# Filling matmuls in a backward recurrence, and four moves of copies and loads in its forward recurrence

One core of one Trainium2 chip (trn2). The metric is the device time of one execution in microseconds (us), lower is better. The kernel before takes 5632.72 us, the median of 3 runs (5621.08 to 5634.92).

## The reference

A block of attention with a carried memory, gated by a feed-forward branch, with the gradients of all its inputs. Cut to what matters here:

```python
def _A_ref(x, mem0, Wq, Wk, Wv, Wo, seg_len):      # S = 2048, Dm = 640, H = 32 heads of 128, M = 8, seg_len = 32
    mem = mem0
    for s in range(n_seg):                          # 64 segments, one after the other
        h = concat([mem, x[segment s]])             # 40 rows
        q, k, v = h @ Wq, h @ Wk, h @ Wv
        p = softmax(mask(q @ k.T * scale))
        o = (p @ v) @ Wo
        mem = o[:, :M]                              # 8 rows go on to the next segment
        outs.append(o[:, M:])
# result: x + A(layernorm(x)) * silu(B(layernorm(x)));  the kernel also returns the gradients of x, mem0 and all weights
```

Only the 8 memory rows depend on the segment before. So the kernel runs two recurrent loops of 64 steps, one forward for the memory rows and one backward for their gradients, and puts the work of the other rows, in units of four heads of three segments ("x units"), into the gaps of each step.

## The kernel before

A step is a chain of matmuls and copies with named gaps W0, W1, W2 and G1 to G6. A function called at each gap adds filling work.

Forward loop, the parts that the change touches:

```python
WARM = dict(G2=1, G3=1, G4=2, G5=1)             # filling matmuls, 512 columns each, result never read
def gap(g):
    FILL(g, t, at, kbatch)
    for i in range(WARM.get(g, 0)):
        nc.tensor.matmul((bA if g == "G4" else bB)[:], k.ident[:], Wq[:, 0, 0:512], start=True, stop=True)
    if g in ("G2", "G5"):                       # transposes of one weight block on PE ...
        wt["u"] = units.pop(0); wt["p"] = bview(bA if g == "G2" else bB, ...); wt["u"][0](wt["p"])
    if g == "G2": turned('v', nc.sync)          # ... and their copy, by VectorE
    if g == "G6": turned('s', nc.sync)          # ... or by ScalarE
def FILL(g, t, at, kbatch):
    if g == "W0":
        ... at(pv, t - 1, 0); at(turn_p, t - 1, 2)
        for u in kb[0:2]: ld_k(*u)              # key rows, two loads on SyncE's queue
    elif g == "W1": at(pv, t - 1, 1)
    elif g == "W2": at(pv, t - 1, 2); ride_ld(t + 1)    # third x unit
    elif g == "G1": oride(t); at(scores, t, 0); at(turn_q, t, 2); ...
    # ... cut ...
def oride(t):                                   # GpSimd: the o rows of the other segment tokens
    nc.gpsimd.tensor_copy(oTm[:, :, 8:32], uu.pop(("o", t))[:])
def pv(tl, qd, q=nc.gpsimd):
    # PE: xot and xpo;  ScalarE: copies xoT and xv, and the issue of xoT's store between them;
    q.dma_start(k.OR[...], v[0:n])              # GpSimd's queue: waits for xv
# the memory chain between the gaps (cut):
#   W2 -> psT matmuls -> sTm copy (ScalarE) -> ride copy (GpSimd) -> gap G1 -> transposes -> msb (VectorE)
#   -> Em = exp (ScalarE) -> Zm, rZm, Pm = Em * rZm (VectorE) -> gap G2 -> transposes of Pm -> PTm -> gap G3
#   -> poms -> oTm (VectorE) -> gap G4 -> projection with Wo -> fold -> next step
```

Backward loop:

```python
WARM = dict(G1=1, G5=2, G6=1)
# gap W1: turn(t, 1) (transposes of the second unit's v and gradient rows), gmem_ld(t + 1, 2)
# gap G3: turn(t, 2), dprob(t, 1);   after it: load_k(t - 1), two pairs of dSm stores
# gap G4: load_xp(t - 1), dsoft(t, 1), gmem_ld(t, 0)
# gap G5: dprob(t, 2), gmem_ld(t, 1)
def gmem_ld(tl, qd):
    gmem(tl, qd)        # last use of a unit's buffers (gkp matmuls), store GXP on SyncE's queue
    ld_next()           # load of the unit four further on: gqv (3 to 5 loads), gor, gPr, SyncE's queue
```

A unit's load reuses the buffers that the `gmem` four units earlier frees. Backward steps have three, three and two units in turn (t mod 3 = 0, 2, 1; t runs from 63 down to 0).

Of the kernel before, what the change touches and what calls it, by code (L numbers as in the profile page):

```python
# [10 lines left out]
F32 = mybir.dt.float32  # L11
# [5 lines left out]
P = 128  # L17
# [385 lines left out]
def phase3_Afwd(k, W4, Wv, Wk_):  # L403
    nc, tc = k.nc, k.tc
# [5 lines left out]
    with tc.tile_pool(name="b0", bufs=1) as io, tc.tile_pool(name="b0s", bufs=3) as stp, \  # L410
# [7 lines left out]
        n = 0  # L418
# [22 lines left out]
    with tc.tile_pool(name="ast", bufs=1) as st, tc.tile_pool(name="achain", bufs=1) as ch, \  # L441
# [247 lines left out]
        def oride(t):  # L689
            if 0 <= t - k.OT0 < k.NO:  # L690
                nc.gpsimd.tensor_copy(oTm[:, :, 8:32], uu.pop(("o", t))[:])

        def pv(tl, qd, q=nc.gpsimd):
            n = k.geo(tl)[3]
            c0 = qd * 512
            v = uu.pop(("v", tl, qd))
            if 4 * tl < k.NO:
                pt = ps.tile([P, 4, 96], F32, name="xot", tag="x", bufs=5)
                for j in range(4):
                    nc.tensor.matmul(pt[:, j, :], v[0:n, j * P:(j + 1) * P], PTs[qd % 2][0:n, j, 24:120], start=True, stop=True)  # L700
                ot = fl.tile([P, 4, 4, 24], BF16, name="xoT", tag="xoT", bufs=2)
                nc.scalar.copy(ot[:].rearrange("p c h t -> p h c t"), pt[:].rearrange("p h (c t) -> p h c t", t=24))
                nc.scalar.dma_start(k.OTX[4 * tl:4 * tl + 4, :, 4 * qd:4 * qd + 4, :].rearrange("c p h t -> p c (h t)"),
                                    ot[:].rearrange("p c h t -> p c (h t)"))
            po = ps.tile([P, 512], F32, name="xpo", tag="x", bufs=5)
            for j in range(4):
                nc.tensor.matmul(po[:, j * P:(j + 1) * P], PTs[qd % 2][0:n, j, :], v[0:n, j * P:(j + 1) * P],
                                 start=True, stop=True)
            nc.scalar.copy(v[0:n], po[0:n])  # L709
            q.dma_start(k.OR[120 * tl:120 * tl + n, c0:c0 + 512], v[0:n])  # L710

# [17 lines left out]
        def turned(eng, q):  # L729
            wt["u"][1](fl.tile([P, DC, P], BF16, name="wTst", tag="wTst"), wt["p"], eng, q)  # L730

        def gap_of(t):
            def at(f, tt, i):
                b = batch.get(tt, ())
                if i < len(b):
                    f(*b[i])

            def gap(g):
                FILL(g, t, at, kbatch)
                for i in range(WARM.get(g, 0)):  # L740
                    nc.tensor.matmul((bA if g == "G4" else bB)[:], k.ident[:], Wq[:, 0, 0:512], start=True, stop=True)

                if g in ("G2", "G5"):
                    wt["u"] = units.pop(0)
                    wt["p"] = bview(bA if g == "G2" else bB, P, DC, P, bf=True)
                    wt["u"][0](wt["p"])
                if g == "G2":
                    turned('v', nc.sync)
                if g == "G6":
                    turned('s', nc.sync)  # L750
            return gap

        def FILL(g, t, at, kbatch):
            kb = kbatch.get(t, ())
            if g == "W0":
                oride_ld(t)
                at(pv, t - 1, 0)
                at(turn_p, t - 1, 2)
                for u in kb[0:2]:
                    ld_k(*u)  # L760
            elif g == "W1":
                at(pv, t - 1, 1)
            elif g == "W2":
                at(pv, t - 1, 2)
                ride_ld(t + 1)
            elif g == "G1":
                oride(t)
                at(scores, t, 0)
                at(turn_q, t, 2)
                for i in range(2):  # L770
                    at(lambda a, b: ld("q", a, b), t + 1, i)
            elif g == "G2":
                at(scores, t, 1)
                at(scores, t, 2)
                for u in kb[0:2]:
                    kprep(*u)
                for u in kb[2:]:
                    ld_k(*u)
                for i in range(3):
                    at(lambda a, b: ld("v", a, b), t, i)  # L780
            elif g == "G3":
                at(soft, t, 0)
                at(soft, t, 1)
            elif g == "G4":
                at(soft, t, 2)
                for i in range(3):
                    at(norm, t, i)
            elif g == "G5":
                at(turn_p, t, 0)
                at(turn_q, t + 1, 0)  # L790
                at(lambda a, b: ld("q", a, b), t + 1, 2)
            elif g == "G6":
                at(turn_p, t, 1)
                at(turn_q, t + 1, 1)
                for u in kb[2:]:
                    kprep(*u)
# [184 lines left out]
def phase4_Abwd(k, out2, WoT, WvT, WkT, WqT, later):  # L981
# [3 lines left out]
    with tc.tile_pool(name="gst", bufs=1) as st, tc.tile_pool(name="gchain", bufs=1) as ch, \  # L985
# [20 lines left out]
        nc.sync.dma_start(k.m_rows(k.GWO, T - 1).rearrange("r (c d) -> (r c) d", d=160),  # L1006
                          goxs[(T - 1) % 2][0:32].rearrange("p a b -> p (a b)"))
        rides = {}
        WARM = dict(G1=1, G5=2, G6=1)

        def ride_ld(t):
            if t < 8:
# [245 lines left out]
        def gap_of(t):  # L1258
# [5 lines left out]
            def gap(g):  # L1264
# [21 lines left out]
                elif g == "G6":  # L1286
                    at(dsoft, t, 2)
                for i in range(WARM.get(g, 0)):
                    nc.tensor.matmul((bA if g[0] == "W" or g == "G1" else bB)[:], k.ident[:], WqT[:, 0, 0:512], start=True, stop=True)
            return gap  # L1290
        todo = pro + todo

# [713 lines left out]
```

## Time and profile before

| | before |
|---|---|
| median time, us | 5632.72 |
| forward loop, first to 64th step start, us | 1354.6 (half speed 68) |
| backward loop, first to 64th step start, us | 1260.6 (half speed 187) |
| mean backward step, us | 20.01 |
| mean granted TensorE clock | 0.946 |

The step starts are the first matmul of each step that reads the carried rows; "half speed" is time at a granted clock of 0.5 in the profile. The granted clock is 1.0 or 0.5 there, nothing between, and it changes on a grid of 3.41 us: of its 186 stretches in the kernel before, all but the last are multiples of 3.413 us. The lines of the profile that carry the argument stand in the prediction: the busy times of the two loops, steps with and without half speed, and the waits in a step.

### The profile page before, as it was taken

How to read it: one execution, taken by the hardware profiler on the slowest of the kernel's cores; microseconds unless marked ns; L12 is line 12 of the kernel's file. 1: busy time of each engine (PE TensorE's matmuls, PEld its weight loads, DVE VectorE, ACT ScalarE, POOL GpSimd, SP SyncE). 2: the span in 40 equal slices, each digit the busy share in tenths (PEclk: the TensorE clock that was granted, in tenths of full speed). 3: DMA queues.
4: the chain of work that ended last, by engine and by line, in shares of the span. 5: the costliest groups of instructions: out<-in, count | busy, mean ns of one | idle time of the engine just before them, and what ended most of it. 6: DMA issues, size and time to landing. Idle time of an engine off the chain costs nothing. (4 is left out here: it accounts for less than half of the span.)

```text
span 5628.0 us, 166669 instructions
## 1 busy us (share of the span) xinstructions
PE 4974.2 (88%) x67201; PEld 3195.0 (57%) x67486; DVE 2378.9 (42%) x7485; ACT 1834.3 (33%) x5040; POOL 1566.2 (28%) x2606
## 2 busy tenths in 40 slices
PE   4988889899888775889888896999999999999999
PEld 2554555555555453556666564665566556657565
DVE  5742555555555423444445442332233223311461
ACT  2432455555555522323333331332223212301111
POOL 0000244444444303333333332342234223300000
PEclk9999999999999787989999997999999999999999
DMA  7563455556555475666666664444344334456332
GB/s 256 181 205 94 140 163 168 167 166 170 161 157 151 113 208 164 177 185 182 188 179 179 174 173 114 120 100 98 84 108 102 99 87 102 122 163 228 102 118 91
DMA packets 1007171, 835.83 MB, mean 149 GB/s; under 512 B 505131, under 2 KB 894919, under 8 KB 1003083
## 3 DMA queue, kind: packets, MB, share of 16 engines
q1 hardware_dynamic: 760275, 570.63, 35.7%
q0 software_dynamic: 92560, 149.71, 9.5%
q10 hardware_dynamic: 153564, 104.81, 6.5%
q8 instruction: 532, 8.72, 0.6%
q14 instruction: 240, 1.97, 0.1%
HBM read 511.81 MB, written 324.39 MB: 149 GB/s over the span
## 5 line engine op out<-in xcount | busy, mean ns | idle before, releaser
L1460 PE MATMUL wg<-gr,hr 120*128 120x512 bf16 (+1 forms) x2640 | 588.1, 384 | 17.3 <-DVE dST L1392 13.2
L1438 PE MATMUL g<-w,gT 128*128 128x320 bf16 x3840 | 547.9, 299 | 0.0
L1460 PEld LDWEIGHTS <-hr 120*128 120x128 bf16 (+1 forms) x2640 | 257.8, 99 | 339.5 <-issue 45.9
L1438 PEld LDWEIGHTS <-gT 128*128 128x128 bf16 x3840 | 368.6, 98 | 136.0
L251 POOL DMA_DIRECT2D r<-GOS x256 | 143.1, 564 | 794.1 <-PE r6p L1402 720.5
L370 PEld LDWEIGHTS <-gkv 128*8 128x8 bf16 x8192 | 213.6, 98 | 152.1 <-DVE gkv L1069 34.4
L90 DVE CAST wgo<-wg 128x512 bf16<-128x512 f32 x72 | 47.5, 687 | 583.3 <-PE wg L1460 292.1
L351 PEld LDWEIGHTS <-hx 128*32 128x32 bf16 x7680 | 180.1, 96 | 182.7 <-issue 30.9
L90 DVE CAST stg<-bank 128x512 bf16<-128x512 f32 x256 | 177.0, 691 | 224.2 <-PE bank L351 213.6
L661 ACT ACTIVATE xP<-xsp,xnm 120x120 bf16<-120x120 f32 (+1 forms) x704 | 239.9, 375 | 32.1 <-issue 25.6
L370 PE MATMUL gbank<-WvT,gkv 128*8 128x320 bf16 x4096 | 225.6, 396 | 27.4 <-DVE gkv L1069 27.4
L1447 DVE TENSOR_TENSOR ghacc<-ghacc,g 128x320 f32<-128x320 f32 x240 | 117.0, 487 | 277.2 <-PE g L1438 277.2
L92 ACT CAST wgo<-wg 128x512 bf16<-128x512 f32 x48 | 25.8, 589 | 635.5 <-PE wg L1460 635.5
L1405 ACT CAST gr<-r6p 120x512 bf16<-120x512 f32 (+1 forms) x176 | 103.1, 586 | 361.2 <-PE r6p L1402 339.6
L1220 POOL DMA_DIRECT2D DSR<-gdS x176 | 101.6, 577 | 419.1 <-DVE gdS L1218 370.1
L710 POOL DMA_DIRECT2D OR<-xv x163 | 93.3, 572 | 444.2 <-ACT xv L709 280.8
L672 POOL TENSOR_TENSOR xP<-xP,xrz 120x480 bf16<-120x480 bf16 x163 | 161.6, 992 | 162.1 <-ACT xP L661 108.0
L92 ACT COPY gT<-t6g 128x960 bf16<-128x960 bf16 (+5 forms) x216 | 166.8, 792 | 118.4 <-PE t6g L1421 117.9
L370 PE MATMUL bank<-Wo,oTm 128*32 128x320 bf16 x4032 | 177.7, 330 | 14.7 <-DVE oTm L579 13.5
L1218 DVE SCALAR_TENSOR_TENSOR gdS<-gdp,Dx,gPr 120x120 bf16<-120x120 f32 (+1 forms) x680 | 182.9, 331 | 0.0
L536 DVE COPY vt<-stg 8x512 bf16<-8x512 bf16 x512 | 166.1, 324 | 31.8 <-ACT stg L92 24.9
L370 PEld LDWEIGHTS <-oTm 128*32 128x32 bf16 x4032 | 138.6, 105 | 64.9 <-issue 41.0
(360 smaller groups left out, 11094.4 us busy)
## 6 DMA issues: line engine op xcount, KB each, us to landing
QVS<-stg SPq DMA_DIRECT2D x128, 256.0 KB
gqv<-QVS SPq DMA_DIRECT2D x108, 192.0 KB
vTt<-VTD SPq DMA_DIRECT2D x64, 320.0 KB
VTD<-gvT POOLq DMA_DIRECT2D x168, 120.0 KB, 3.4
OR<-xv POOLq DMA_DIRECT2D x163, 120.0 KB, 2.8
DSR<-gdS POOLq DMA_DIRECT2D x168, 112.5 KB, 3.2
dS<-DSR SPq DMA_DIRECT2D x168, 112.5 KB
P<-PR SPq DMA_DIRECT2D x168, 112.5 KB
```

The lines of the kernel that those rows point to most:

```text
L90: return nc.vector.tensor_copy(out, in_)
L92: return nc.scalar.copy(out, in_)
L251: eng.dma_start(d, src if src.shape[0] > 1 else src[0])
L351: k.nc.tensor.matmul(bank[32 * g:32 * g + 32, :], x[:, dc, :], W[:, dc, c0:c0 + 512], start=(dc == 0), stop=(dc == k.DC - 1), tile_positio ...
L370: k.nc.tensor.matmul(pm[p0:p0 + nq, 0:320], x[:, h, :], W[:, h, 320 * b:320 * b + 320], start=(first and i == 0), stop=(last and i == 15), ...
L536: nc.vector.tensor_copy(vt[p0:p0 + 8, c0:c0 + 512], sv[32 * g:32 * g + 8, b * 512:(b + 1) * 512])
L661: nc.scalar.activation(Pb[0:n, j, 0:n], sp[0:n, j, :], ACT.Exp, bias=nmx[0:n, j:j + 1], scale=k.scale, accum_out=Z[0:n, j:j + 1])
L672: eng.tensor_tensor(Pb[0:n, :, 0:n], Pb[0:n, :, 0:n], bc_last(rz[0:n], n), ALU.mult)
L1218: nc.vector.scalar_tensor_tensor(dS[0:n, j, :], dp[0:n, j, :], Dx[0:n, j:j + 1], Pr[0:n, j, :], op0=ALU.subtract, op1=ALU.mult)
L1438: nc.tensor.matmul(pg[:], ring[:, i, j, r0:r0 + P], Ws[qd][i][:, j, 320 * h:320 * h + 320], start=(i == 0 and j == 0), stop=(i == 2 and j ...
L1447: nc.vector.tensor_tensor(a if qd < 7 else gx[:, 320 * h:320 * h + 320], a, g[h][:], ALU.add)
L1460: nc.tensor.matmul(accs[dc][:], hr[0:n, tl, dc * P:(dc + 1) * P], st["g", NTL * qd + tl, i][0:n, :], start=(tl == 0), stop=(tl == NTL - 1))
```

## The change

In the backward loop, matmuls that compute nothing used are to keep PE busy enough for its full clock. In the forward loop, four moves: VectorE's copy of a weight block goes behind the softmax starts; the third unit's copies go behind the memory scores' copy; ScalarE's copy of a weight block goes ahead of the q and k copies of G6; key rows are loaded after the key store.

```diff
@@ forward loop
+        def pv_mm(tl, qd):      # the matmuls of pv
+        def pv_out(tl, qd, q=nc.gpsimd):    # xoT copy and store, xv copy and store
             def gap(g):
+                if g == "G6":
+                    turned('s', nc.sync)
                 FILL(g, t, at, kbatch)
+                if g == "G3":
+                    turned('v', nc.sync)
                 ... filling matmuls, weight transposes ...
-                if g == "G2":
-                    turned('v', nc.sync)
-                if g == "G6":
-                    turned('s', nc.sync)
         def FILL(g, t, at, kbatch):
                 at(turn_p, t - 1, 2)
+            elif g == "W1":
                 for u in kb[0:2]:
                     ld_k(*u)
-            elif g == "W1":
                 at(pv, t - 1, 1)
             elif g == "W2":
-                at(pv, t - 1, 2)
+                at(pv_mm if t < T else pv, t - 1, 2)
             elif g == "G1":
+                at(pv_out, t - 1, 2)
                 oride(t)
@@ backward loop
-        WARM = dict(G1=1, G5=2, G6=1)
+        WARM = dict(W1=3, G1=2, G2=2, G5=2, G6=1)
-                    nc.tensor.matmul((bA if g[0] == "W" or g == "G1" else bB)[:], ...
+                    nc.tensor.matmul((bA if g in ("W1", "G1", "G2") else bB)[:], ...
```

The rest of the diff splits `pv` into `pv_mm` and `pv_out`.

More of the change, by code (lines that the diff above doesn't have):

```diff
@@ L693, in pv @@
         def pv(tl, qd, q=nc.gpsimd):
+            pv_mm(tl, qd)
+            pv_out(tl, qd, q)
+        def pv_mm(tl, qd):
             n = k.geo(tl)[3]
-            c0 = qd * 512
-            v = uu.pop(("v", tl, qd))
+            v = uu["v", tl, qd]
             if 4 * tl < k.NO:
@@ L700, in pv @@
                     nc.tensor.matmul(pt[:, j, :], v[0:n, j * P:(j + 1) * P], PTs[qd % 2][0:n, j, 24:120], start=True, stop=True)
+                uu["pt", tl, qd] = pt
+            po = ps.tile([P, 512], F32, name="xpo", tag="x", bufs=5)
+            for j in range(4):
+                nc.tensor.matmul(po[:, j * P:(j + 1) * P], PTs[qd % 2][0:n, j, :], v[0:n, j * P:(j + 1) * P],
+                                 start=True, stop=True)
+            uu["po", tl, qd] = po
+        def pv_out(tl, qd, q=nc.gpsimd):
+            n = k.geo(tl)[3]
+            c0 = qd * 512
+            v, po = uu.pop(("v", tl, qd)), uu.pop(("po", tl, qd))
+            if 4 * tl < k.NO:
+                pt = uu.pop(("pt", tl, qd))
                 ot = fl.tile([P, 4, 4, 24], BF16, name="xoT", tag="xoT", bufs=2)
@@ L704, in pv @@
                                     ot[:].rearrange("p c h t -> p c (h t)"))
-            po = ps.tile([P, 512], F32, name="xpo", tag="x", bufs=5)
-            for j in range(4):
-                nc.tensor.matmul(po[:, j * P:(j + 1) * P], PTs[qd % 2][0:n, j, :], v[0:n, j * P:(j + 1) * P],
-                                 start=True, stop=True)
             nc.scalar.copy(v[0:n], po[0:n])
@@ L1288, in gap @@
                 for i in range(WARM.get(g, 0)):
-                    nc.tensor.matmul((bA if g[0] == "W" or g == "G1" else bB)[:], k.ident[:], WqT[:, 0, 0:512], start=True, stop=True)
+                    nc.tensor.matmul((bA if g in ("W1", "G1", "G2") else bB)[:], k.ident[:], WqT[:, 0, 0:512], start=True, stop=True)
             return gap
```

## The prediction

> **What bounds the kernel now.** I read the page first, then the granted clock by stage, then single steps of the two recurrent loops, the waits in each loop, and the timelines of ACT and PE inside a step. Each loop has 64 steps, every one fed by the step before, so a loop costs 64 times its step.
>
> The busy times and clock of the forward loop (first row) and the backward loop (second); the columns are time, busy us of PE, PEld, DVE, ACT and POOL (instruction counts in brackets), granted PE clock, DMA share, GB/s:
> ```profile
> 542.60:1907.00 1364.40, 1225.12 (x22711) 764.23 (x22836) 763.65 (x2228) 737.19 (x2455) 550.69 (x783) 0.98 0.55 158
> 2205.50:3470.00 1264.50, 1126.41 (x24102) 749.08 (x24229) 589.78 (x2769) 378.13 (x1227) 419.01 (x765) 0.93 0.63 170
> ```
> See the clock: 0.98 forward, 0.93 backward. Now five successive steps of the backward loop, cut where the first matmul of a step starts, and below them two neighbouring stretches of 3.41 us inside the fifth, and two pairs of such stretches elsewhere:
> ```profile
> 3027.67:3046.15 18.48, 16.39 (x379) 11.29 (x381) 9.95 (x50) 5.60 (x19) 6.44 (x13) 1.00 0.63 175
> 3046.15:3064.97 18.82, 16.77 (x386) 11.63 (x389) 8.60 (x41) 6.38 (x20) 6.62 (x13) 1.00 0.70 184
> 3064.97:3085.23 20.26, 18.38 (x395) 12.36 (x398) 10.30 (x53) 6.68 (x22) 7.13 (x14) 0.92 0.67 191
> 3085.23:3105.23 20.00, 17.91 (x379) 11.65 (x382) 10.04 (x50) 5.60 (x19) 6.43 (x13) 0.91 0.64 181
> 3105.23:3125.74 20.51, 18.45 (x386) 12.34 (x389) 8.70 (x41) 6.39 (x20) 6.61 (x13) 0.92 0.59 157
> ...
> 3109.24:3112.66 3.42, 2.14 (x54) 1.76 (x58) 1.22 (x5) 1.57 (x5) 1.29 (x2) 1.00 0.77 237
> 3112.66:3116.07 3.41, 3.41 (x60) 1.94 (x56) 2.80 (x17) 0.00 (x0) 0.21 (x1) 0.50 0.58 165
> ...
> 3051.22:3054.63 3.41, 2.74 (x75) 2.05 (x76) 1.62 (x8) 0.63 (x2) 0.47 (x1) 1.00 0.56 176
> 3054.63:3058.04 3.41, 3.41 (x96) 2.68 (x92) 3.35 (x24) 1.68 (x5) 1.26 (x3) 1.00 0.84 256
> ```
> See two things. A step at full clock takes 18.5 or 18.8 us; one in which the clock stood at one half for 3.41 us takes 20.0 to 20.5. And the half-speed stretch follows a stretch with little PE work: 2.14 us busy, against 2.74 where the clock stayed. I sorted all 3.41 us stretches of the loop so: nearly all that led to half speed had under about 2.45 us of PE, and 42 of 46 began 2.5 to 4.3 us into the step. There PE waits three times (a step at full clock, us and length first, idle time and its releaser last):
> ```profile
> 3050.77 1.00 PE L1090 MATMUL gbank<-gmT,vTt 128*40 128x8 bf16 x32 [0.89 <-DVE gmT L1085]
> 3052.49 0.29 PE L1067 MATMUL gbank<-bdP,gOst 128*128 128x128 bf16 x2 [0.23 <-ACT gOst L1098]
> 3053.36 0.31 PE L370 MATMUL gbank<-WvT,gkv 128*8 128x320 bf16 x4 [0.43 <-DVE gkv L1069]
> ```
> These are the ends of gaps W1, G1 and G2, where the change puts its fillers. The forward loop is bound by a chain PE, ACT, DVE. ACT in a step with three x units, one early in the loop, then the waits of the whole forward loop that matter (us, times, longest):
> ```profile
> 1151.90 0.49 ACT L702 CAST xoT<-xot 128x384 bf16<-128x384 f32 x1
> 1152.41 0.37 ACTq L703 DMA_DIRECT2D OTX<-xoT  x1
> 1152.95 0.58 ACT L709 CAST xv<-xpo 120x512 bf16<-120x512 f32 x1 [0.57 <-DMA OR<-xv]
> 1153.43 0.36 ACT L543 CAST sTm<-bank 40x256 bf16<-40x256 f32 x1
> 1153.70 0.55 ACT L631 COPY xqT<-qpt 128x480 bf16<-128x480 bf16 x1
> 1154.72 0.27 ACT L557 ACTIVATE Em<-msb 128x80 bf16<-128x80 f32 x1 [0.47 <-DVE msb L555]
> ```
> ```profile
> ACT stg L92 <- DMA KS<-stg: 17.9, 19, 2.2
> PE bank L351 <- ACT wTst L92: 9.6, 38, 0.6
> ```
> The memory scores end on PE at 1152.76, but their copy sTm starts at 1153.43, behind the third unit's two copies and a DMA issue. The value stage buffer waits 19 times for the key store, and the second key half 38 times for the weight transpose's copy.
>
> [...] a window need not be idle, 2.1 to 2.4 us of PE in 3.41 was too little. [...] two forward fillers in a row start 0.22 us apart here. [...] The key store lands 2.0 to 2.5 us after its issue in the first steps and mostly 3 to 6 us later on, with the loads ahead.
>
> **Backward loop.** Added per step: three fillers in W1, one more in G1, two in G2; 6 x 0.22 = 1.3 us of PE. They stand at the end of their gap, so they run while PE waits. W1: the time free before the wait ends is 0.85 us with three units (a gap then holds eight more small matmuls), 1.04 with two; three fillers take 0.65, so they fit. G2: free 0.57, needed 0.43, fits. G1: free 0.38 before any filler, one filler is there already (its record is missing), two take 0.43, so 0.05 us falls on the path.
> What it wins: windows beginning 2.5 to 4.3 us into the step have 2.06 to 2.63 us of PE and gain at least 0.6, so pass 2.45. Of 63 step intervals (mean 20.01, sum 1260.5), the 14 at full clock average 18.69, the 45 with a half-speed stretch of 3 us or more 20.46. By the position in the tile, full-clock steps are 18.83, 18.83 and 18.47, mean 18.71. If all were so: 63 x (20.01 - 18.71) = 82 us. Taken off: 4 for the two steps of 24.0 and 23.4 us that wait for bulk DMA, 3 for half speed left at the loop's ends, 3 for G1 (64 x 0.05), 4 for steps in which PE comes late to W1 (4 of 64 have 0.07 to 0.18 us free; taken as 8 x 0.5). Sum: **-68 us**.
>
> **Forward loop**, by parts; each is an estimate from the lines of a step:
> - Weight copy of G2 moved behind the two softmax starts. DVE's copy is 0.48 us and stands ahead of the maxima that let the exponentials start. In steps with three units the last exponential ends 0.75 us after the projection, and the fold waits for it (18.50 against 17.75 us into the step). Exponentials then start about 0.4 earlier, limited by PTm's copy on ACT. 14 early first-in-tile steps x 0.4 = 5.6, 14 late ones x 0.35 = 5.
> - Third unit's copies behind sTm. sTm starts 0.63 earlier, but ACT now has xoT, its DMA issue, xv and xqT (about 2.2 us from start to start) between sTm and Em, where before it had xqT alone and 0.47 us idle. In three-unit steps Em comes about 0.3 later, and xqT later still, so PE waits for it before the third scores; with the part above such a step gains only about 0.15: 14 x 0.15 = 2. In two-unit steps there is no xqT; Em comes 0.14 earlier: 2. In the last third of the loop there is no xoT and sTm isn't held up: 0.
> - Weight copy of G6 ahead of the q and k copies: bank B is free before the next step; 38 waits, **9.6**, each on PE's path.
> - Key loads behind the key store: the store should land about 1 to 1.5 us earlier. Nine late steps and two early ones with late landings are 1 to 3 us longer than their neighbours (two with half speed besides): 13.
> Sum 5.6 + 5 + 2 + 2 + 9.6 + 13 = **-37 us**. Nothing outside the two loops changes. Total: 5632.7 - 68 - 37 = **5528 us**, 1.9% faster.
>
> **Rivals.** (a) Fillers on the path: if PE were the bound in the gaps, 64 x 1.3 = 83 us would eat all; time near 5600. Against: the three waits name DVE and ACT. (b) The clock doesn't recover, because the threshold moves or another stretch (16 to 18 us into the step, at 2.65 to 2.8) falls under it: -30 backward, 5565. Against: full-clock steps run three in a row with those same stretches. (c) The ACT queue turns the third unit's move into a loss: Em 0.5 to 0.7 later in 14 to 28 steps, some 15 us, with more half-speed windows there; forward -15, total 5550. [...] (d) Key store and softmax parts are larger and forward half speed (69 us of it now) shrinks too: forward -60, total 5500.
>
> **Range and chances.** The backward part can't pass 82 and with (a) in part is at least 50; forward lies between -10 and -60. Ends rarely meet: 5500 to 5562. The 2% line is 5520, so faster 0.38, within 2% 0.61, slower 0.01.
>
> **What would show it.** Right: clock of the backward loop at 0.98 or more, steps of 18.5 to 18.9 us, no idle before the three matmuls above; the wait for the weight copy gone and the one for the key store under 5 us; sTm right after the scores. Wrong: clock still 0.95, or full-clock steps over 19.1 (fillers on the path). Em later in three-unit steps shows (c). The forecast fails most likely by the size of the key store's part.

## The result

The changed kernel takes 5587.68 us (median of 4 runs, 5578.57 to 5590.96), beside 5631.07 for the kernel before on the same chip. The ratio is 0.9923, with a 95% interval of 0.9906 to 0.9941. (Ratios here are the mean time of one kernel's fast runs over the mean of the other's of the same rounds, so not quite the ratio of the medians.) That is 43 us where 105 were predicted, and outside the range of 5500 to 5562.

Line numbers past L690 are shifted by the diff: L702, L709, L710 are now L718, L721, L722, the backward loop's numbers are 13 higher. The busy times of the two loops in the changed kernel, same columns as in the prediction, each window from the first step's start to the end of the loop:
```profile
540.10:1891.50 1351.40, 1215.11 (x22712) 740.70 (x22838) 774.12 (x2228) 739.81 (x2455) 553.76 (x783) 0.97 0.56 159
2188.70:3419.50 1230.80, 1140.65 (x24423) 749.07 (x24610) 586.80 (x2769) 379.85 (x1227) 419.52 (x765) 0.98 0.64 175
```
The backward clock went from 0.93 to 0.98, as intended. The backward loop is 34 us shorter (1226.8), the forward loop 13 (1341.6); the time outside the loops changed by 4 us.

Three successive backward steps of the changed kernel, and one other:
```profile
2839.90:2858.80 18.90, 17.93 (x393) 12.01 (x396) 8.62 (x41) 6.39 (x20) 6.63 (x13) 1.00 0.71 187
2858.80:2877.70 18.90, 18.11 (x399) 12.21 (x403) 10.21 (x53) 6.69 (x22) 7.13 (x14) 1.00 0.73 195
2877.70:2896.25 18.55, 17.55 (x384) 11.57 (x387) 9.97 (x50) 5.61 (x19) 6.44 (x13) 1.00 0.71 196
2698.92:2726.14 27.22, 20.83 (x383) 12.87 (x387) 10.04 (x50) 5.86 (x19) 7.37 (x14) 0.81 0.63 180
```
The first three, 18.90, 18.90 and 18.55, repeat through most of the loop: full clock, and only 0.07 us above the full-clock steps of before (18.83, 18.83, 18.47). The last, step 37, took 27.22 us at a clock of 0.81. There are five such steps of over 21 us besides 51 and 52, which are left out because two large GWO<-GS copies are issued there in both kernels. PE's waits in the first of these steps (idle time and releaser last):
```profile
2844.53 1.00 PE L1103 MATMUL gbank<-gmT,vTt 128*40 128x8 bf16 x32 [0.26 <-DVE gmT L1098]
2846.86 0.38 PE L1302 MATMUL gbank<-WqT,ident 128*128 128x512 bf16 x1 [0.16 <-issue]
2857.86 0.55 PE L398 MATMUL gbank<-sel,fsum 64*128 64x8 bf16 x5 [0.30 <-DVE fsum L382]
```
Of the three waits that the prediction showed, 0.89, 0.23 and 0.43 us, one is left with 0.26: the fillers stand in them.

Forward, the waits that the prediction named, and a new one (us, times, longest):
```profile
PE bank L757 <- DVE wTst L90: 26.9, 60, 0.5
...
PE bank L351 <- ACT wTst L92: 4.8, 5, 1.5
ACT stg L92 <- DMA KS<-stg: 3.9, 6, 1.1
```
The wait for ScalarE's weight copy went from 38 times to 5, that for the key store from 17.9 us to 3.9. Both are what the prediction asked for. The new one: the two fillers of G4 (L757) write the bank that VectorE's weight copy reads, and the copy is later now.

ScalarE in step 28 of the changed kernel, which answers to the ScalarE lines in the prediction:
```profile
1149.86 0.37 ACT L543 CAST sTm<-bank 40x256 bf16<-40x256 f32 x1 [0.79 <-PE bank L541]
1150.13 0.47 ACT L718 CAST xoT<-xot 128x384 bf16<-128x384 f32 x1
1151.11 0.59 ACT L721 CAST xv<-xpo 120x512 bf16<-120x512 f32 x1 [0.51 <-ACT xoT L718]
1151.59 0.56 ACT L631 COPY xqT<-qpt 128x480 bf16<-128x480 bf16 x1
1152.04 0.28 ACT L557 ACTIVATE Em<-msb 128x80 bf16<-128x80 f32 x1
```
sTm now waits for PE alone, and the third unit's copies follow it: the move did what it says. But Em now stands straight behind xqT with no idle time, where in the prediction's lines ScalarE had idled 0.47 us before it. Over steps 3 to 41, Em started 0.03 us after its input msb in the kernel before; in the changed kernel it starts 0.66 us after it in steps with t mod 3 = 1 and 0.38 us in those with 2. ScalarE's queue now holds it up, as the prediction's rival (c) feared.

Where, then, did the forward gain go? The next two fences are the same place of step 29, before and after: GpSimd's copy of the o rows (L691), VectorE's Pm (L563), and the PE transposes that wait for Pm (L568).
```profile
1176.71 0.83 POOL L691 COPY oTm<-oride 128x768 bf16<-128x768 bf16 x1
1177.62 0.24 DVE L563 TENSOR_TENSOR Pm<-Em,rZm 128x80 bf16<-128x80 bf16 x1
1177.92 0.24 PE L568 MATMUL bank<-ident,Pm 128*40 128x128 bf16 x2 [0.30 <-DVE Pm L563]
```
```profile
1173.55 0.53 POOL L722 DMA_DIRECT2D OR<-xv  x1 [3.45 <-ACT Em L557]
1173.93 1.09 DVE L563 TENSOR_TENSOR Pm<-Em,rZm 128x80 bf16<-128x80 bf16 x1
1174.08 0.84 POOL L691 COPY oTm<-oride 128x768 bf16<-128x768 bf16 x1
1175.07 0.23 PE L568 MATMUL bank<-ident,Pm 128*40 128x128 bf16 x2 [1.47 <-DVE Pm L563]
```
GpSimd's copy stands behind the third unit's store in its queue, and it starts as that store ends (within 0.01 us in all 24 steps of 3 to 41 with both, in the changed kernel). That store now waits longer, because xv comes later. (The view names Em as the releaser; but in steps 3 to 41 of both kernels the store starts 0.29 to 0.30 us after the end of xv.) So the copy has slid beside Pm, and Pm takes 1.09 us instead of 0.24 on the chain that ends each step. Then PE, which had 0.30 us of idle time here, has 1.47, and the clock follows. Two successive stretches of that step in the changed kernel, by the columns of the prediction:
```profile
1173.18:1176.59 3.41, 1.57 (x40) 1.11 (x40) 3.00 (x8) 2.19 (x10) 2.45 (x4) 1.00 0.57 149
1176.59:1180.00 3.41, 2.96 (x34) 1.33 (x37) 1.15 (x5) 2.17 (x14) 1.86 (x3) 0.50 0.51 177
```
1.57 us of PE work in the first, half speed in the second. Over steps 3 to 41 (before the last third, where there is no xoT), the means by step type (first, second and third type from here on; the third unit of the step before is finished in the second and third type) are:

| steps 3 to 41, mean us | t mod 3 = 0 | 1 | 2 |
|---|---|---|---|
| step before | 21.32 | 22.14 | 21.22 |
| step after | 20.49 | 21.81 | 22.80 |
| Pm before | 0.26 | 0.24 | 0.24 |
| Pm after | 0.24 | 0.60 | 1.01 |

The third type, with the 1.01 us Pm, is the one with two units and lost 1.6 us a step; the prediction gave it a gain.

And the backward loop? These are step 37's PE lines for its second unit, with the load it waits for (cut from the timeline of that step):
```profile
2701.79 1.09 SPq L283 DMA_DIRECT2D gor<-GOS  x1
...
2704.73 0.37 PE L1199 MATMUL gvpt<-ident,gqv 120*128 120x120 bf16 x4 [2.51 <-DMA gqv<-QVS]
...
2707.71 0.58 PE L1206 MATMUL ggpt<-ident,gor 120*128 120x120 bf16 x4 [2.61 <-DMA gor<-GOS]
```
The gor part of the load was issued at 2701.79, when the step was already 2.87 us old (its first part at 0.52 us), and PE stood idle twice for 2.5 us until the rows came; then the clock fell, for 10.2 us of the step. In quiet steps with t mod 3 = 1 or 2 the second unit's load begins some 16 us into the step before, and its gor rows land 0.1 to 2.2 us ahead of their use.

### The profile page after: what moved, and what is told of

Same layout as the page of the kernel before. It is cut to its first block, busy times and chain, and to the rows that moved or that the text cites. A ratio compares the mean times of both kernels' runs of the same rounds, so it can differ in the third digit from the quotient of the medians.

```text
span 5576.9 us, 167295 instructions
## 1 busy us (share of the span) xinstructions
PE 4983.0 (89%) x67526; PEld 3173.1 (57%) x67870; DVE 2387.1 (43%) x7485; ACT 1839.2 (33%) x5040; POOL 1569.9 (28%) x2606
## 5 line engine op out<-in xcount | busy, mean ns | idle before, releaser
L370 PEld LDWEIGHTS <-gkv 128*8 128x8 bf16 x8192 | 189.9, 87 | 105.5 <-DVE gkv L1082 26.3
L722 POOL DMA_DIRECT2D OR<-xv x163 | 93.8, 576 | 432.7 <-ACT xv L721 340.1
L1434 PE MATMUL t6g<-ident,gr 120*128 120x120 bf16 (+1 forms) x2112 | 171.8, 221 | 3.6 <-DVE wgo L90 3.1
L351 PE MATMUL gbank<-WoT,gox 128*32 128x512 bf16 x2560 | 154.1, 388 | 22.8 <-POOL gox L1037 19.4
L1302 PE MATMUL gbank<-WqT,ident 128*128 128x512 bf16 x453 | 155.1, 391 | 19.2 <-issue 11.2
```

Source lines behind the costliest of these rows:

```text
L351: k.nc.tensor.matmul(bank[32 * g:32 * g + 32, :], x[:, dc, :], W[:, dc, c0:c0 + 512], start=(dc == 0), stop=(dc == k.DC - 1), tile_positio ...
L370: k.nc.tensor.matmul(pm[p0:p0 + nq, 0:320], x[:, h, :], W[:, h, 320 * b:320 * b + 320], start=(first and i == 0), stop=(last and i == 15), ...
L1302: nc.tensor.matmul((bA if g in ("W1", "G1", "G2") else bB)[:], k.ident[:], WqT[:, 0, 0:512], start=True, stop=True)
L1434: nc.tensor.transpose(pt[:, i - i0, j, :], st["g", u, i][0:n, j * P:(j + 1) * P], k.ident[0:n, 0:n])
```

## The experiments

"Forward" and "backward" are the times from the first to the 64th step start in the profiled run. "Long" counts backward steps over 21 us, without the first and without 51 and 52. Ratios are to the kernel before.

| run | median us | ratio (95%) | forward | backward | long |
|---|---|---|---|---|---|
| the change | 5587.68 | 0.9923 (0.9906-0.9941) | 1341.6 | 1226.8 | 5 |
| e1 backward only | 5601.61 | 0.9948 (0.9932-0.9963) | 1347.5 | 1236.9 | 8 |
| e2 forward only | 5635.89 | 1.0001 (0.9987-1.0015) | 1341.6 | 1273.2 | 3 |
| e3 third unit back | 5579.90 | 0.9902 (0.9886-0.9919) | 1323.7 | 1238.4 | 7 |
| e4 o copy in G2 | 5641.74 | 1.0012 (0.9997-1.0026) | 1383.5 | 1237.1 | 8 |
| e5 loads on ScalarE | 5655.15 | 1.0051 (1.0036-1.0066) | 1345.7 | 1304.7 | 19 |
| e6 before, loads on ScalarE | 5679.57 | 1.0093 (1.0079-1.0108) | 1348.0 | 1315.0 | 20 |
| e7 e3 and e5 | 5637.48 | 1.0019 (1.0000-1.0037) | 1317.8 | 1304.2 | 18 |
| e8 e7 and G3=3 | 5619.53 | 0.9986 (0.9971-1.0002) | 1297.4 | 1312.1 | 21 |
| e9 early gkp | 5575.37 | 0.9887 (0.9862-0.9911) | 1352.1 | 1208.0 | 3 |
| e10 e3 and G3=3 | 5562.97 | 0.9872 (0.9856-0.9887) | 1303.0 | 1232.9 | 5 |
| e11 e9 and e10 | 5529.30 | 0.9809 (0.9789-0.9828) | 1301.6 | 1205.7 | 3 |
| e12 e3, key loads back | 5586.78 | 0.9905 (0.9872-0.9938) | 1326.9 | 1240.2 | 8 |
| e13 o copy ahead of store | 5575.73 | 0.9899 (0.9883-0.9915) | 1320.8 | 1232.7 | 6 |
| e14 e3, first weight copy back | 5575.75 | 0.9894 (0.9879-0.9909) | 1317.6 | 1228.6 | 7 |
| e15 e3, second weight copy back | 5596.55 | 0.9931 (0.9915-0.9948) | 1340.4 | 1252.3 | 10 |
| e16 e11, xp first, shorter queue | 5497.98 | 0.9760 (0.9746-0.9775) | 1300.1 | 1184.2 | 1 |
| e17 e16, third unit as changed | 5499.51 | 0.9766 (0.9750-0.9782) | 1308.8 | 1185.0 | 1 |
| e18 e16, first weight copy back | 5502.82 | 0.9781 (0.9760-0.9801) | 1309.8 | 1183.3 | 0 |

How far one profile can be trusted: the forward code of the change also runs in e2, e5 and e9, and gave 1341.6, 1341.6, 1345.7 and 1352.1; that of the kernel before runs in e1 and e6, 1354.6, 1347.5 and 1348.0. So a forward difference below some 10 us between two profiles is not a finding by itself. The spread is smaller where there is less half speed: e3 and e7 share their forward code (1323.7, 1317.8), and so do e8, e10, e11 and e16 (1297.4 to 1303.0). The nine kernels with the change's backward loop give 1226.8 to 1252.3, mean 1236.2; the two with that of before give 1260.6 and 1273.2.

### Each loop alone: e1 and e2

e1 is the kernel before with the two backward lines of the diff; e2 is the changed kernel with those two lines undone.

> The kernel before with only the six more fillers per backward step. Theory A (fillers restore the clock, but steps of 18.9 us outrun the loads on the sync queue, and seven long stalls give part back): backward loop about 34 us shorter as in the changed kernel, total about 5597, clock of the loop 0.97 or more, again several steps of over 21 us. Rival B (the stalls of the changed kernel are chance or come from the forward change): backward loop 60 us or more shorter, total under 5570.

> The changed kernel with the old fillers in the backward loop. Theory A: the forward part alone gives 10 to 17 us, total about 5617, and the two-unit steps of the first two thirds again take 22.6 us with a half-speed stretch. Rival B (the forward part is worth 35 us or more, and something in the backward loop hides it): total under 5600.

e1 wins 0.5%, some 29 us; e2 wins nothing. Each loop's shortfall thus shows with that loop changed alone. (29 and 0 are less than the 43 of both together, but the intervals allow for it.) By the means over equal code, the forward part is worth 5 us (1350.0 to 1345.3) and the backward part 31 (1266.9 to 1236.2).

### Forward: third unit's copies put back, and the o copy moved on: e3 and e4

```diff
 # e3, on the changed kernel
-                at(pv_mm if t < T else pv, t - 1, 2)
+                at(pv, t - 1, 2)
-                at(pv_out, t - 1, 2)
 # e4, on the changed kernel: oride(t) from the gap G1 to the gap G2
```

> The changed kernel with the third x unit's copies put back ahead of the scores' copy sTm. Theory A (the move makes GpSimd's copy of the oride rows start 1.1 us later after Em's start, beside DVE's Pm, which then takes 1.09 in place of 0.24 us, and the idle PE loses its clock): Pm is 0.24 us again, two-unit steps fall from 22.6 to about 20.8 us, total about 25 us less than the changed kernel, 5562. Rival B (the 22.6 us steps come from the weight copy moved to G3, or from the later key loads): they stay at 22.6 and the total is within 5 us of the changed kernel or above.

> The changed kernel with GpSimd's oride copy moved from G1 to G2, behind Pm's store on GpSimd, so that it cannot run beside Pm or the vt copies. Theory A: Pm is 0.24 us in all steps, two-unit steps about 20.3, three-unit steps 0.4 less, total about 40 us less than the changed kernel, 5547. Rival B (Pm is slow for another reason): no change of Pm, total within 5 us of the changed kernel. A middle outcome, 5560, would mean that the copy now collides with the oTm copies.

In e3 Pm takes 0.24 to 0.28 us on average in every type again, and the forward loop is 18 us shorter (e7, with the same forward code, 24). The third unit's move was a loss. e4 was meant to keep the move and take the GpSimd copy away from Pm. Pm did fall to 0.24, but the copy met another VectorE instruction, and the loop got longer by 42 us. That instruction in all e4's steps, then one meeting in the timeline:
```profile
L657 DVE TENSOR_SCALAR xnm<-xmx x146: 169/171/1391, 702.5 to 1898.7; 120x4 f32<-120x4 f32 x146
```
```profile
1200.42 1.32 DVE L657 TENSOR_SCALAR xnm<-xmx 120x4 f32<-120x4 f32 x1
1200.87 0.84 POOL L691 COPY oTm<-oride 128x768 bf16<-128x768 bf16 x1
```
A 0.17 us instruction on four columns took 1.32 us, to the end of the GpSimd copy. So the collision is not bound to Pm: xnm is held up in the same way. It doesn't hold for every VectorE instruction: in the changed kernel rZm stands wholly inside the copy 23 times and takes 0.17 us, as it does alone, and in the kernel before Zm does so 27 times with 0.24, while Pm in the changed kernel has a median of 0.63 us in 37 meetings (0.24 alone). What makes an instruction one that is held up was not shown.

### Forward: the same move with GpSimd's order mended: e13

```diff
             elif g == "G1":
-                at(pv_out, t - 1, 2)
                 oride(t)
+                at(pv_out, t - 1, 2)
```

> The changed kernel with one line moved: GpSimd's copy of the o rows (oTm<-oride) is issued ahead of the third unit's store instead of behind it, the third unit's copies stay behind the memory scores' copy. Theory: GpSimd runs in order, so in the changed kernel its copy waits behind a store that waits for the third unit, falls beside the Pm multiplication of VectorE and holds it up. Then Pm falls back to 0.24 us in all types, the early three-unit and second-type steps lose the 0.4 to 1.0 us and the half-speed windows that follow, and the forward loop falls from 1341.6 to 1323 or below, ratio near 0.990. Rival: the third unit's copies themselves delay the path, whatever GpSimd does: forward stays at 1338 or more although Pm is 0.24. A third outcome is that the earlier copy meets another two-operand copy of VectorE (vt, L536), as it did in one type of step before: then vt grows from 0.29 to 0.8 us and the gain is half.

The line that shows Pm in all steps of e13, and one step:
```profile
L563 DVE TENSOR_TENSOR Pm<-Em,rZm x60: 241/241/244, 617.3 to 1858.8; 128x80 bf16<-128x80 bf16 x60
```
```profile
1174.03 0.24 DVE L563 TENSOR_TENSOR Pm<-Em,rZm 128x80 bf16<-128x80 bf16 x1
1174.32 0.24 PE L568 MATMUL bank<-ident,Pm 128*40 128x128 bf16 x2 [0.83 <-DVE Pm L563]
```
The longest Pm is 0.244 us, and the forward loop is 1320.8, as short as with the copies put back (1323.7, and 1317.8 in e7). So the harm came from the place of GpSimd's copy in its queue.

It doesn't show what the third unit's move is worth by itself, since the copy of the o rows has met another instruction. The third outcome of the expectation came true too; VectorE and GpSimd earlier in the same step of e13:
```profile
1169.26 3.41 DVE L536 COPY vt<-stg 8x512 bf16<-8x512 bf16 x8
1169.90 0.83 POOL L691 COPY oTm<-oride 128x768 bf16<-128x768 bf16 x1
1172.70 0.24 DVE L553 TENSOR_REDUCE mmx<-bank 128x2 f32<-128x80 bf16 x1
```
A vt copy takes 0.28 us, so eight of them 2.3 and not 3.41; those that meet the o copy take 1.31 us (median); such long ones stand in 41 steps of e13, against 18 of e3. mmx, the first step of the memory softmax, then starts behind the last vt copy: over steps 3 to 41, 0.35 us after its input in the second type and 0.48 in the third, against 0.11 in e3. And in the second type Em still waits 0.41 us for ScalarE. Together they make Em 0.35 us later than in e3 in the second type, and no earlier in the third, though sTm is some 0.5 us earlier; second-type steps are 21.62 us against 21.14. An order in which GpSimd's copy meets neither Pm nor vt was not tried.

### Forward: the other parts, each put back on e3: e12, e14, e15

e12 puts the key loads back into W0, e14 VectorE's weight copy back to the end of G2, e15 ScalarE's weight copy back to the end of G6.

> The changed kernel with the third unit's copies put back (e3) and the key rows' loads put back to the head of the gap W0, ahead of the key store, as in the kernel before. The prediction gave this part 13 us (0.6 us of earlier key store in some 21 steps with two key units). If that is right, the forward loop goes from 1323.7 to about 1335 us. If the earlier key store is not on the path, it stays within 3 us of 1323.7, and the gain of e3's forward loop belongs to the two weight copies.

> e3 (third unit's copies put back) with the first weight copy put back from G3 to the end of G2, ahead of the softmax. The prediction gave this part 10.6 us (5.6 early, 5 late: Em no longer held up by the 0.7 us copy). If right: forward from 1323.7 to 1334, ratio from 0.990 to 0.992. If the copy was off the path, forward within 3 us of 1323.7.

> e3 with the second weight copy put back from the head of G6 to its end. The prediction gave this part 9.6 us (PE's wait for the bank at the step's start: 38 waits, 9.6 us together). If right: forward from 1323.7 to 1333 and the wait of PE L351 on ACT wTst back at about 0.25 us in some 38 steps. If another wait takes its place, within 3 us of 1323.7.

Key loads: 3.2 us, under the spread, where 13 were predicted. The wait of ScalarE for the key store came back (12.2 us against 5.1 in e3, from the wait lists), so the wait was real but mostly not on the path. Second weight copy: 16.7 us, more than the predicted 9.6; the wait of PE for it came back at 39 times and 13.2 us. First weight copy: putting it back didn't make the loop longer (6 us shorter than e3, the same as e7). By type the reason shows: 20.91, 21.70 and 20.45 us a step against 20.42, 21.14 and 21.77 in e3. Two types lost 0.5 us, as the prediction reckoned; the third won 1.3, and its half-speed time went from 27 us to 0.

### Forward: the clock held by two more fillers: e10 and e18

e10 is e3 with `WARM = dict(G2=1, G3=3, G4=2, G5=1)`; e18 is e16 (below), which has these fillers too, with the first weight copy back at the end of G2.

> Forward loop: the changed kernel with the third unit's copies put back to the gap W2 and two more filling matmuls in G3 (three instead of one). Expected from the runs with loads on ScalarE's queue, where these two fillers took the forward loop from 1317.8 to 1297.4 us: forward 1297 to 1303 against 1341.6 of the changed kernel and 1323.7 with the copies put back alone, half-speed time in the forward loop below 15 us, no Pm of over 0.3 us; backward as in the changed kernel (1227 to 1238). Whole kernel 5540 to 5560, ratio 0.984 to 0.988. If the fillers' gain there came from the moved loads and not from the clock, forward stays at 1318 or more and the ratio at 0.990.

> e16 with the first weight copy put back to the end of G2. If its new place is worth the predicted 10.6 us when no half speed blurs it: forward from 1300 to 1310 or more, steps of the first two types 0.4 to 0.5 us longer, ratio 0.978. If PE's wait for the copy in G4 (0.45 us a step, 60 times) gives the gain back: forward within 4 us of 1300, that wait gone, and ratio 0.975 to 0.977.

e10 lands where it was expected: forward 1303.0, half speed 16.5 us in all, ratio 0.9872. With the clock out of the way, e18 gives the first weight copy its price: forward 1309.8 against 1300.1, types 20.82, 21.68, 20.59 against 20.47, 21.20, 20.93. That is 10 us, close to the predicted 10.6 and outside the 1297.4 to 1303.0 of the four profiles with e16's forward code; it is one profile, and the intervals of the two ratios overlap. My alternative, that PE's new wait in G4 eats the gain, misses: the wait did go in e18 (PE waits for oTm instead, 13.5 us in 48 times), but only the third type got shorter by it.

### Backward: how early the loads are issued: e5 to e8

The suspicion: SyncE's queue is the limit, as it issues 29 transfers in a step, which take 16.0 us of it (steps 60 to 20; 28 and 15.2 over the loop). These runs gave the gor and gPr loads to ScalarE's queue.

```diff
-  k.load_x(gor, ..., nc.scalar if early and i > 3 else nc.sync);  nc.sync.dma_start(Pr[0:n], ...)
+  k.load_x(gor, ..., nc.scalar if not early or i > 3 else nc.sync); (nc.sync if early else nc.scalar).dma_start(Pr[0:n], ...)
```
e5 is this on the changed kernel, e6 on the kernel before, e7 on e3, e8 on e7 with G3=3.

> The changed kernel with the backward loop's loads of gor and gPr issued by ACT in place of the sync queue (same bytes, six issues a step moved). Theory A (the long backward steps come from the order of the sync queue: the second unit's load is issued behind the key rows, which wait for PE, the two small DSR stores, xp and GXP, some 19 us into the step, and lands 0 to 2 us before its use): no step over 21 us but those at t = 52 and 51, backward loop of 63 steps 1195 us or less in place of 1227 to 1238, total 5550 to 5560. Rival B (DMA bandwidth: the bytes do not fit into 18.9 us steps): the long steps stay, backward loop over 1220, total within 5 us of the changed kernel.

> The kernel before with the same six issues moved to ACT. Theory A (in the kernel before the half clock made steps of 20.5 us, so the load was in time): no more than 8 us gained, median backward step still 20.1 to 20.5. Rival C (the late loads also cause the half clock of the kernel before, and the fillers were not needed): backward loop under 1230 and total under 5600.

> The changed kernel with the third unit's copies put back and the gor and gPr loads on ACT. If both causes are as told and add up: 8 us for the first and about 32 for the second, total 5545. Under rival B it stays at 5580.

> The same with three fillers in place of one in gap G3 of the forward loop. Two-unit steps of the forward loop wait about 0.5 us for the copy PTm there, and in 8 of 13 of them the clock went to one half after a 3.41 us stretch with 2.29 us of PE. Theory A (the clock follows the PE time of a stretch of 3.41 us): that half-speed time falls from 27 us to under 10, early two-unit steps from 21.8 to about 20.8, total 15 us less than without. Rival D (the fillers lengthen the path to the projection): three-unit steps longer by 0.3 us or more and the total no better.

SyncE's issue time fell to 13 us a step, and the loops got worse: 18 to 21 long steps, backward 1304 to 1315, also with the fillers of before (e6). What SyncE's queue waits for in e5:
```profile
SPq L1053 <- PE gbank L1140: 126.5, 50, 4.3
SPq L1249 <- DMA krow<-KS: 57.8, 40, 3.1
SPq L1187 <- DMA gor<-GOS: 50.4, 38, 2.7
```
The second and third lines are waits for landings; in the changed kernel all such waits of the queue together are some 15 us. They came with splitting a unit's loads over two queues, and PE's matmuls waited 36 us for gqv from QVS (24 times), against 6.4 (6 times) in the changed kernel. So e5 to e8 do not tell "queue too long" from "load too late". What they do show is that this split of the loads over two queues added waits for landings. e8's forward loop (1297.4) gave the idea for e10.

### Backward: the load issued sooner: e9 and e11

```diff
                 elif g == "G3":
                     at(turn, t, 2)
                     at(dprob, t, 1)
+                    at(gmem_ld, t, 0)
                 elif g == "G4":
                     ...
-                    at(gmem_ld, t, 0)
```
This frees the buffers earlier, so that the load goes ahead of the key row in the queue. e11 is e10 with it.

> The changed kernel with one move in the backward loop: the memory-row gradient of a step's first unit (gkp matmuls), which frees that unit's buffers and is followed by the load of the next step's unit, goes from the gap G4 to the end of G3. The load then enters the SyncE queue ahead of the key row instead of behind the key row, two dSm stores and xp: some 4 us sooner (10.3 instead of 14.4 us into the step), so that the second unit's rows land about 6 us ahead of their use instead of 0 to 2. Theory A, the long steps are loads issued too late for the second unit of steps with t mod 3 = 1 or 2 (all long steps but 51 are of these): the long steps of 21 us and more go, except 52 and 51 which lie beside the two large gate-to-GWO copies; time from first to last backward step start 1226.8 -> 1190 to 1198, whole kernel some 30 us below the changed kernel, ratio to the kernel before about 0.987. Theory B, the DMA engines cannot carry the loads in steps of 18.9 us whenever they are issued: long steps stay in number (7 or more), backward within 8 us of 1226.8, ratio 0.992. Rival C, the moved gkp or the key row issued 3.5 us later costs PE a wait in each step: median step up from 18.90 to 19.2 or more.

> Third unit's copies put back, three fillers in G3, and the early gkp of e9 together. If the two causes are independent the gains add: forward 1297 to 1303, backward 1190 to 1200, whole kernel 5505 to 5530, ratio 0.978 to 0.982. If the long steps are DMA-bound (theory B), backward 1225 to 1240 and ratio 0.985 to 0.988.

PE's waits in the backward loop for the landing of unit rows, in the changed kernel:
```profile
PE gvpt L1199 <- DMA gqv<-QVS: 6.4, 6, 2.5
PE gvpt L1199 <- DMA gqv<-QVX: 5.4, 3, 2.6
...
PE ggpt L1206 <- DMA gor<-GOS: 3.9, 4, 2.6
PE ggpt L1206 <- DMA gor<-GX: 3.2, 4, 1.2
```
In e9 and e11 the same list has no such line for PE's matmuls. From its first issue to its use, the second unit's load has 7.6 us (median) in e9's steps with t mod 3 = 1 and 9.7 in those with 2; in the changed kernel it has 5.3 and 6.8. Backward is 1208.0 and 1205.7, below all nine kernels with late loads. Not all of that is the loads: the move also made the median step shorter, 18.69 against 18.90 us, which makes some 13 us in 63 steps. The kind of step is telling too. The load of the second unit is late only in steps with t mod 3 = 1 or 2; in the others it is issued 14 to 19 us ahead of its use. Of the 64 long steps in those nine profiles, 45 have t mod 3 = 1, 19 have 2, and none has 0. If the transfers were too slow whenever issued (theory B), steps with 0 would be among them. Theory A stands. It gave 1190 to 1198, though. Part of the rest was of my own making, as VectorE's waits in e11 say:
```profile
DVE gkv L1081 <- DMA xp<-GXP: 47.2, 12, 5.8
```
The move had put the unit load ahead of the xp load too. All three of e11's long steps (36, 33, 21) have t mod 3 = 0, steps that were never long in those nine profiles, and VectorE waits 5.2 to 5.7 us for xp in each.

### The rest of the queue, and what the third unit is worth then: e16 and e17

```diff
 # e16, on e11
+                    load_xp(t - 1)          # in G3, ahead of gmem_ld(t, 0)
                     at(gmem_ld, t, 0)
-                        (nc.sync, nc.gpsimd)[a].dma_start(k.DSR...
+                        nc.gpsimd.dma_start(k.DSR...
 # e17, on e16: third unit's copies as in the change, oride(t) ahead of pv_out
```

> e11 with the load of xp put ahead of the unit load in G3 and the second pair of dSm stores on GpSimd's queue instead of SyncE's (1.3 us less issue time on SyncE in each step). In e11 VectorE waited 5.2 to 5.8 us for xp in steps 51, 36 and 21 and the SyncE queue was 16.0 us issuing in steps of 18.7. If the queue's length is what is left: those waits go, long steps only at 52 and 51, backward 1205.7 to 1195, whole kernel some 8 to 12 us below e11, ratio 0.979. If not: backward within 4 us of 1205.7 and ratio 0.981.

> e16 with the third unit's copies left behind the memory scores' copy, as the change has them, and GpSimd's copy of the o rows ahead of the third unit's store, as in e13. The prediction said 0.14 us a two-unit step for this move, and nothing or a loss for the three-unit ones. If the move is worth its early sTm (10.35 against 11.43 us into the step), forward falls from 1300 to 1293 or below and the ratio to 0.974 or below; if the path through PE's fillers hides it, forward stays within 3 us of 1300 and the ratio at 0.975 to 0.977.

The two loops of e16, by the columns of the prediction:
```profile
544.90:1854.90 1310.00, 1207.27 (x22840) 732.43 (x22964) 760.87 (x2228) 739.93 (x2455) 551.42 (x783) 1.00 0.59 164
2150.70:3338.90 1188.20, 1115.90 (x24423) 747.61 (x24610) 586.38 (x2769) 374.17 (x1227) 494.06 (x891) 0.99 0.67 181
```
e16 is the fastest version: 5497.98 us, 2.4% below the kernel before. It was expected at 0.979 and came out better: backward 1184.2, one long step, no wait of VectorE for xp. e16 changes two things at once, so how much the xp order and how much the shorter queue gave stays open. e17 misses both of its expectations for the forward loop: 1308.8, neither below 1293 nor within 3 us of 1300.1. It doesn't price the third unit's move alone either. The vt copies are held up as in e13 (in 48 steps), Em is 0.28 us later than in e16 in the second type (21.62 us a step against 21.20), and in the third type 17 us of half speed are back, where e16 has none: the clock was not held. As written, with GpSimd's copy in either place, the move wins nothing in any run here.

## Why the prediction was wrong, point by point

**Backward: fillers bring back the clock (82 us at most).** Right. Half-speed time fell from 187 to 49 us, and the quiet steps are 18.90, 18.90, 18.55, so the fillers cost 0.07 us a step on the path (0.05 predicted). e16, where little else disturbs, wins 76 us against the predicted 68, though some 13 of these are the shorter steps that came with e9's move. The prediction's reading of the clock was a little too sharp: redone over the whole loop, 47 stretches of 3.41 us at full clock were followed by half speed; they held 1.60 to 2.64 us of PE, eight of them more than 2.45, and ten stretches with 2.41 to 2.47 kept the clock.

**Backward: what was taken off.** This step failed, at the term "4 for steps in which PE comes late to W1". It asked whether PE leaves the fillers room in W1. It did not ask whether W1's own input, the second unit's rows, still comes in time when the step is 1.3 us shorter. The long steps cost 36 us on average (the excess over 18.8 us of the 64 long steps, over nine profiles), and 68 less 36 is the 31 to 34 that was measured. The kernel before shows where to look: its list of PE's waits in the backward loop already has landings of unit rows in it, with a few tenths of a us each:
```profile
PEld L1186 <- DMA gqv<-QVS: 2.5, 6, 0.4
...
PE ggpt L1193 <- DMA gor<-GOS: 1.4, 2, 0.8
```
A step that is shorter on PE leaves the same transfer less time: in steps with t mod 3 = 1, which are most of the long ones, the second unit's load had 6.0 us from its first issue to its use (median), and has 5.3 in the changed kernel; in those with 2 it is 6.8 in both. And the late landing cost twice in step 37: PE stood idle twice for 2.5 us, and 10.2 us at half speed came with it. That the lateness is the cause is shown by e9 and e11.

**Forward: third unit's copies behind sTm (a gain of 2 + 2 us predicted).** This step failed in sign: e3 and e13 say that it cost some 20 us. The prediction counted ScalarE's queue, and rightly: against e3, Em is 0.36 us later in the second type (about 0.3 predicted) and 0.15 earlier in the third (0.14 predicted). It left out GpSimd, whose store waits for the copies that moved and whose next instruction then collides with Pm. Shown by e13, where a change of GpSimd's order alone brings Pm back to 0.24 us and wins 21 us. Rival (c) gave about the right total for forward, -15, and its mechanism is there, but smaller than it said: Em 0.36 us later in the 13 early second-type steps, not 0.5 to 0.7 in 14 to 28. The larger part is the collision.

**Forward: key loads (13 us).** The wait went from 17.9 to 3.9 us as predicted, the gain was 3 (e12), not to be told from nothing. From issue to landing the store took 3.73 us before and 2.97 in the changed kernel (medians of steps 4 to 63), so 0.8 less where 1 to 1.5 were estimated. The prediction named this term as the likeliest to fail.

**Forward: first weight copy (10.6 us).** Right with the clock held, as far as one profile tells (10 us, e18), hidden otherwise: in e3 half speed in the third type of step took the gain (e14).

**Forward: second weight copy (9.6 us).** Under-estimated: 17 us (e15), part of it perhaps spread.

**The sum.** Predicted 37 forward; 5 to 13 measured. Putting the collision (about 20) back gives 25 to 33. What is then still missing is the key loads and the half speed in the third type of step, which three fillers in G3 remove (e10: 21 us).

## What to carry to other kernels

When an instruction is moved on one engine, follow everything that waits for it into the queues of the other engines, and look at what stands behind it there: here a GpSimd copy of 0.83 us, beside which Pm took 1.09 us instead of 0.24. When steps get shorter, list the transfers by their margin, landing to use: those with less margin than the step will lose can become the new bound, as the gor rows did here (0.1 to 2.2 us of margin, steps 1.3 us shorter), and the mean hides them because only some steps stall (64 in nine profiles). A gain in order can be taken back by the clock (the first weight copy: no gain against e14, 10 us against e18), so price each part with the clock held.

## What the profiles leave open

- The order of the records does not tell which engine is held up. In the changed kernel Pm's record starts 0.15 us *before* GpSimd's copy in 12 of the 13 steps of the third type from 8 to 44 (in the one shown, 1173.93 against 1174.08), and 0.45 us before in e4's xnm (1200.42 against 1200.87), and each time VectorE's instruction was the longer for it, to 0.11 us or less after the copy's end (Pm ends at 1175.02, the copy at 1174.92). No run here shows when the two were issued, and the profile's own legend calls spans on GpSimd rough.
- Here GpSimd's copy is not longer for a collision with Pm or xnm, 0.83 to 0.84 us (0.82 to 0.89 over all copies of the changed kernel), nor is it with vt (0.83 us, the median of 16). The whole cost falls on VectorE.
- How much PE work keeps the clock was not shown. 1.57 us of it in a stretch of 3.41 led to half speed, in the backward loop of before 1.60 to 2.64, while 2.90 did not (e10, in the same step). As stretches from 2.41 us on also kept the clock in that backward loop, and in the forward loop of before from 1.99 on, the profile's busy time gives no sharp limit.
